# Second attention layer: QKV groups and transpositions of its first two chunks placed in another order

## Chip, core and metric

The kernel runs on one core of one Trainium2 chip. The metric is device time in microseconds (us) of one execution. Times before: 1803.42, 1805.32 and 1803.96 us in three runs, median 1803.96.

## What is computed

`x` is 2048 x 640 floats. Four layers follow one another, each of the form x = x + f(layernorm(x)): attention, Fourier mixing, attention, Fourier mixing.

```python
# attention, layers 0 and 2: 32 heads of 20
qkv = x @ wqkv
idx = pos[:, None] - 2 * arange(8)             # 8 keys, 2 rows apart
logits = einsum("bhsd,bhswd->bhsw", q, k[idx]) * 20 ** -0.5
o = einsum("bhsw,bhswd->bhsd", softmax(logits), v[idx])
y = o @ wo
# mixing, layers 1 and 3
y = dft_seq_re @ (x @ dft_hid_re.T) - dft_seq_im @ (x @ dft_hid_im.T)
```

The change concerns layer 2, the second attention, alone.

## The kernel before

**Tiling.** The rows of x lie in four chunks c (0 to 3) of 512 rows, and each chunk in four tiles j (0 to 3) of 128 rows. The QKV product is cut into 64 groups g: (c, q, j) is chunk, quarter q of the heads, tile. A group is 15 matmuls of 128x480 (`qkv_mm`, L356): every float operand is held as a high and a low part, and three products of five blocks each are summed. Group g writes PSUM bank m0 when g is even and m1 when g is odd, so a group needs its bank emptied by ScalarE first (`qkv_evac`, L363, into the staging tile `stg`, two buffers, two groups per buffer). After each second group the staging tile is stored to HBM: k and v to `kvb` (L372), q to `qb` (L373) (`qkv_store`; the first stores of the layer go by ScalarE's queue, the others by SyncE's, SP).

**Units.** Attention itself runs on VectorE and GpSimd in 32 units u, unit u taking chunk u // 8 and half a quarter of the heads; each unit takes two steps, 2u and 2u + 1. In step s VectorE multiplies q by the keys (`qk_mul`, L425), GpSimd folds the product (L427), VectorE reduces it (L433); ScalarE takes the exponentials of a unit in step 2u + 2 (`soft_exp`, L441); three steps after its L425 VectorE multiplies by the values (`av_mul`, L463) and GpSimd adds the eight products (L478 to L480). A unit reads keys and values as windows from `kvb` (`w_load`, L411) and its q from `qb` (`q_load`, L395), both by SP. `qs` has one buffer; ScalarE copies it into PSUM (`q_copy`, L398, in step 2u - 1), and VectorE's L425 of step 2u waits for that copy.

**Chunks 1 to 3.** Each tile of x is loaded (`x_load`, L189, tag `xa`, two buffers), normalised by ScalarE (`x_norm`, L185, one step ahead of its transposition) and transposed by TensorE (`tp`: transpositions L321, the high part copied by ScalarE L325, subtracted by TensorE L329, the low part copied by ScalarE L344). The output product (`wo_mm`, L503) of chunks 0 and 1 lies between.

**What sets the order.** All of it is written out by hand. `layer_a` puts every piece of work into a plan under a step (from -7 to 66) and a phase, and then issues steps in order and, in each step, the phases of `PHASES` in order. Each engine runs its own instructions in that order, SP its DMAs as well, and a later instruction of an engine never passes an earlier one that waits. The step of group g is `gs[g]`: the first 16 (chunk 0) are listed in `LEAD2`, the others follow from a loop over steps that also sets `tx`, the step in which tile (c, j) is transposed. A group's evacuation stands in the step after it, phase `evac`, if its step is under 6 or odd; in its own step, phase `evacA`, if it is the first of an even step; and in the step after, phase `evacO`, if it is the second. For ScalarE the phases of a step come in the order `evac`, `hi` (L325), `exp` (L441), `evacA`, `actL` (L344), `evacO`, `actl` (L185), `qc` (L398). For SP: `dma` (x_load, q_load), `evac` (early stores), `dmaw` (w_load), `dmas` (weights of the output product, L565, and later stores).

Of the kernel before, what the change touches and what calls it, by code (L numbers as in the profile page):

```python
# [27 lines left out]
NC = 4  # L28
NJ = 4
# [12 lines left out]
LNS = ((40, 52), (40, 52))  # L42


LEAD2 = (-7, -6, -5, -4, -2, 0, 0, 1, 1, 2, 3, 4, 4, 6, 6, 7)
ZTHIRDS = (
    {49: 3, 50: 3, 51: 2, 53: 3, 54: 1, 56: 3, 57: 6, 58: 3, 59: 4, 60: 2, 61: 1, 62: 3, 63: 4, 64: 1, 55: 0, 52: 0},
    {49: 3, 50: 3, 51: 3, 52: 1, 53: 1, 54: 1, 55: 1, 56: 4, 57: 4, 58: 3, 59: 3, 60: 1, 61: 1, 62: 4, 63: 2, 64: 4},
# [25 lines left out]
def tile_layers(ctx: ExitStack, tc: tile.TileContext, x, wqkv, wo, cs, wre, wim, out):  # L74
# [161 lines left out]
    def layer_a(li, stats, handoff, prev):  # L236
        xin, xout = xs[li], xs[li + 1]
        first = li == 0
# [19 lines left out]
        def at(step, phase, fn, *args):  # L258
            plan.setdefault((step, phase), []).append((fn, args))
# [32 lines left out]
        def tp(step, kind, c, j, k0, k1, bank, col=0, tag=None):  # L292
            if step not in pieces:
                pieces[step] = []
                at(step, "peT0", pc_pe, step)
                at(step, "hi", pc_hi, step)
                at(step, "peL", pc_sub, step)
                at(step, "actL", pc_lo, step)
            pieces[step].append((kind, c, j, k0, k1, bank, col, tag))
# [386 lines left out]
        ]  # L686
        gs = list(LEAD0 if first else LEAD2)
        tx = {(0, j): -8 for j in range(NJ)}
        st = 4
        while len(gs) < NGRP:  # L690
            if st % 2 == 0 and len(tx) < NC * NJ:
                c, j = divmod(len(tx), NJ)
                used = [i for i, x in enumerate(order) if x[0] == c - 1 and x[2] == j]
                if used[-1] < len(gs) and gs[used[-1]] < st:
                    tx[(c, j)] = st
            cap = 0 if st < 6 else 2 if st % 2 == 0 and st not in THIN[ly] else 1
            for _ in range(max(0, cap - gs[:16].count(st))):
                if len(gs) < NGRP and len(gs) <= 16 + st and tx.get(order[len(gs)][::2], st) < st:
                    gs.append(st)
            st += 1  # L700
        for g, cqj in enumerate(order):
            st = gs[g]
# [26 lines left out]
        for c in range(1, NC):  # L729
            for j in range(NJ):  # L730
                b = tx[(c, j)]
                at(b - 4, "dma", x_load, c, j)
                if first:
                    at(b - 3, "actl", x_stats, c, j)
                    at(b - 2, "fin", x_fin, c, j)
                at(b - 1, "actl", x_norm, c, j)
                tp(b, "x", c, j, 0, 4, "xt", 0, f"s{j}")
                tp(b, "x", c, j, 4, 5, "t1", 256)
# [538 lines left out]
    st0 = [None] * NC  # L1277
    b1, b2 = LayerB(1), LayerB(3)
    layer_a(0, st0, b1, None)
    st2 = [None] * NC  # L1280
    b1.run(st2)
    layer_a(2, st2, b2, b1)
    b2.run(None)
    b2.ytile(NT - 1, 0, None)
# [56 lines left out]
```

## Time and profile before

| | |
|---|---|
| median of the runs | 1803.96 us |
| the profiled execution's own time | 1805.26 us |
| its span on the core | 1803.4 us |
| what lies around the span | 1.9 us |
| granted TensorE clock over the span | 0.994 |
| TensorE busy | 1743.7 us, 97% |
| VectorE busy | 1382.3 us, 77% |
| GpSimd busy | 633.5 us, 35% |
| ScalarE busy | 816.8 us, 45% |

Layer 2's attention lies in about 890 to 1250 us of the span. In the views below, PE is TensorE (PEld its weight loads), DVE VectorE, ACT ScalarE, POOL GpSimd, SP SyncE, and SPq the DMAs that SP issues. A row of the timeline has the start in us, the length in us, engine, line, operation, the program's names (out <- in), shapes and how many instructions were merged; in square brackets stands how long the engine had been idle before, and which instruction released it. A row of the table by stretches has the stretch, its length, the busy time of each engine with the number of instructions, the granted clock, the share of DMA engines busy and GB/s. The chain of waits gives start, length and what the end of the program waited for.

### The profile page before, as it was taken

How to read it: one execution, taken by the hardware profiler on the slowest of the kernel's cores; microseconds unless marked ns; L12 is line 12 of the kernel's file. 1: busy time of each engine (PE TensorE's matmuls, PEld its weight loads, DVE VectorE, ACT ScalarE, POOL GpSimd, SP SyncE). 2: the span in 40 equal slices, each digit the busy share in tenths (PEclk: the TensorE clock that was granted, in tenths of full speed). 3: DMA queues.
4: the chain of work that ended last, by engine and by line, in shares of the span. 5: the costliest groups of instructions: out<-in, count | busy, mean ns of one | idle time of the engine just before them, and what ended most of it. 6: DMA issues, size and time to landing. Idle time of an engine off the chain costs nothing.

```text
span 1803.4 us, 26465 instructions
## 1 busy us (share of the span) xinstructions
PE 1743.7 (97%) x8798; PEld 1505.7 (83%) x8798; DVE 1382.3 (77%) x2129; ACT 816.8 (45%) x1702; POOL 633.5 (35%) x591
## 2 busy tenths in 40 slices
PE   9999997989999999999999999999899999999999
PEld 6878896877888888888888889878787888888888
DVE  5999899887767767767739987889777676676673
ACT  5654544444445445445523434444534443443441
POOL 3899898950000000000018987899300000000000
PEclk9999998999999999999999999999999999999999
DMA  6896667847777787777647766687687766866861
GB/s 238 280 312 209 211 202 245 273 166 280 261 253 254 247 269 253 240 269 256 224 134 232 258 191 194 204 307 260 205 300 264 251 222 228 266 231 221 261 208 52
DMA packets 271849, 425.15 MB, mean 236 GB/s; under 512 B 22592, under 2 KB 150592, under 8 KB 271456
## 3 DMA queue, kind: packets, MB, share of 16 engines
q1 hardware_dynamic: 268512, 421.49, 70.5%
q10 hardware_dynamic: 3200, 1.97, 0.4%
q8 instruction: 70, 1.15, 0.3%
q14 instruction: 67, 0.55, 0.1%
HBM read 338.23 MB, written 85.14 MB: 235 GB/s over the span
## 4 chain that ended last, share of the span: by engine, by line
PE 64%; DVE 13%; DMA 9%; POOL 7%; issue 3%; ACT 3%; SPq 0%; DVEq 0%; ACTq 0%; POOLq 0%
PE m L356 15%; PE aux L1018 12%; PE t L1107 10%; PE m L1107 10%; PE pq L1107 5%; PE xt L1107 5%; PE aux L503 4%; DMA win<-cs_in 3%; DVE pr L425 2%; POOL pr L478 2%; DVE pr L463 2%; DMA xc<-stg 2%; POOL pr L427 2%; POOL r L876 1%; POOL pr L479 1%
## 5 line engine op out<-in xcount | busy, mean ns | idle before, releaser
L356 PE MATMUL m<-r,s 128*128 128x480 f32 x1920 | 438.3, 383 | 7.5 <-ACT stg L363 2.9
L356 PEld LDWEIGHTS m<-r,s 128*128 128x128 f32 x1920 | 355.9, 188 | 63.4 <-ACT stg L363 4.6
L1100 ACT CAST r<-win 128x512 fp32r<-128x512 f32 x248 | 151.6, 620 | 170.4 <-DVE win L1136 79.9
L168 POOL TENSOR_TENSOR stats<-stats,mhalf 128x1 f32<-128x1 f32 (+1 forms) x40 | 28.8, 719 | 564.5 <-ACT stats L164 564.5
L1018 PE MATMUL aux<-r2a,zo 128*128 128x320 f32 x768 | 226.4, 309 | 0.0
L478 POOL TENSOR_TENSOR pr<-pr 128x640 f32<-128x640 f32 x126 | 205.6, 1632 | 40.1 <-DVE pr L463 39.2
L1018 PE MATMUL aux<-pr,zo 128*128 128x320 f32 x704 | 208.2, 308 | 0.0
L425 DVE TENSOR_TENSOR pr<-pq,win 128x1280 f32<-128x1280 f32 x128 | 189.8, 1483 | 23.4 <-ACT pq L398 23.3
L1101 DVE TENSOR_TENSOR r<-win,r 128x512 fp32r<-128x512 f32 x248 | 167.3, 687 | 45.6 <-ACT r L1100 43.9
L463 DVE TENSOR_TENSOR pr<-pq,win 128x1280 f32<-128x1280 f32 x128 | 190.8, 1491 | 4.3
L427 POOL TENSOR_TENSOR pr<-pr 128x640 f32<-128x640 f32 x128 | 183.5, 1434 | 19.1 <-DVE pr L425 16.1
L1107 PE MATMUL m<-r,r 128*128 128x512 f32 x606 | 156.5, 392 | 1.0 <-DVE r L1101 0.9
L1018 PEld LDWEIGHTS aux<-r2a,zo 128*128 128x128 f32 x768 | 144.1, 188 | 2.0
L940 PE MATMUL m<-s,r 128*128 128x512 f32 x384 | 120.0, 400 | 16.6 <-DMA s<-c0b 5.3
L1107 PEld LDWEIGHTS m<-r,r 128*128 128x128 f32 x606 | 113.5, 188 | 26.9 <-DVE r L1101 1.2
L1018 PEld LDWEIGHTS aux<-pr,zo 128*128 128x128 f32 x704 | 132.2, 188 | 2.1
L1107 PE MATMUL t<-r,r 128*128 128x512 f32 x483 | 130.7, 393 | 2.1 <-issue 2.1
L940 PE MATMUL t<-s,r 128*128 128x512 f32 x384 | 118.1, 395 | 2.3 <-DVE ot L1000 1.5
L479 POOL TENSOR_TENSOR pr<-pr 128x320 f32<-128x320 f32 x126 | 113.7, 903 | 9.9
L363 ACT COPY stg<-m 128x480 f32<-128x480 f32 x128 | 71.1, 556 | 100.7 <-PE m L356 89.9
L433 DVE TENSOR_REDUCE lg<-pr 128x64 f32<-128x640 f32 x128 | 103.9, 812 | 13.8 <-POOL pr L427 13.6
L1107 PEld LDWEIGHTS t<-r,r 128*128 128x128 f32 x483 | 90.5, 188 | 23.6 <-issue 1.5
(274 smaller groups left out, 3231.2 us busy)
## 6 DMA issues: line engine op xcount, KB each, us to landing
win<-cs_in SPq DMA_DIRECT2D x354, 256.0 KB, 4.1
r<-xc SPq DMA_DIRECT2D x240, 256.0 KB, 4.2
win<-kvb SPq DMA_DIRECT2D x96, 440.0 KB, 4.7
xa<-cs_in SPq DMA_DIRECT2D x122, 256.0 KB, 3.9
win<-kvb SPq DMA_DIRECT2D x64, 360.0 KB, 5.1
xc<-stg SPq DMA_DIRECT2D x40, 512.0 KB, 4.6
kvb<-stg SPq DMA_DIRECT2D x60, 320.0 KB, 3.2
xr<-xs SPq DMA_DIRECT2D x40, 320.0 KB, 3.9
```

The lines of the kernel that those rows point to most:

```text
L356: nc.tensor.matmul(mt[g][:, : 3 * F], st[:, a, k], wq[q][:, b, k], start=n == 0, stop=n == 14)
L425: nc.vector.tensor_tensor(pr, q, wview(u, jp, 0, [[1, FE]]), op=ALU.mult)
L427: nc.gpsimd.tensor_tensor(pv[:, :, 0:10], pv[:, :, 0:10], pv[:, :, 10:20], op=ALU.add)
L433: nc.vector.tensor_reduce(lgs[u][:, 2 * jp : 2 * jp + 2].rearrange("p j w h -> p (j w h)"), prq.pop((u, jp))[:, :, 0:10], axis=AX.X, op=AL ...
L463: nc.vector.tensor_tensor(pr.rearrange("p j w (h d) -> p j w h d", d=DH), lgs[u][:, 2 * jp : 2 * jp + 2].unsqueeze(4).to_broadcast([P, 2, ...
L478: g.tensor_tensor(pr[:, :, 0:4], pr[:, :, 0:4], pr[:, :, 4:8], op=ALU.add)
L479: g.tensor_tensor(pr[:, :, 0:2], pr[:, :, 0:2], pr[:, :, 2:4], op=ALU.add)
L940: self.last = nc.tensor.matmul(self.z[t][k], self.xn[c][:, a, j, k * P : (k + 1) * P], self.ct[s][:, b], start=s == 0 and i == 0, stop=s = ...
L1018: self.last = nc.tensor.matmul(self.ym[e][:, :320], zt[(k, a, ri)][:, j2 * P : (j2 + 1) * P], w[:, e * 320 : (e + 1) * 320], start=(k, a, ...
L1100: nc.scalar.copy(hi, raw)
L1101: nc.vector.tensor_tensor(lo, raw, hi.bitcast(F32), op=ALU.subtract)
L1107: nc.tensor.matmul(bank, w(a, kb), hl[b], start=start and (a, b) == (0, 0), stop=stop and (a, b) == (1, 0),)
```

## The change

The core of the diff:

```diff
-LEAD2 = (-7, -6, -5, -4, -2, 0, 0, 1, 1, 2, 3, 4, 4, 6, 6, 7)
+LEAD2 = (-7, -6, -5, -4, -2, -1, 0, 0, 1, 2, 3, 4, 4, 5, 6, 7)
...
-            if st % 2 == 0 and len(tx) < NC * NJ:
+            if (st % 2 == 0 if first or st > 10 else st > 4 and st != 6) and len(tx) < NC * NJ:
...
-                at(b - 4, "dma", x_load, c, j)
+                at(max(b - 4, tx.get((c, j - 2), 0)), "dma", x_load, c, j)
```

What follows from it in layer 2 (layer 0 is as before):

| | before | after |
|---|---|---|
| steps of groups 5, 7, 13 | 0, 1, 6 | -1, 0, 5 |
| steps of groups 14, 15 | 6, 7 | 6, 7 |
| steps of groups 16 to 24 | 8, 9, 10, 10, 11, 13, 14, 14, 15 | 6, 8, 8, 9, 10, 10, 11, 12, 13 |
| groups done by the end of step 21 | 0 to 31 | 0 to 34 |
| groups done by the end of step 33 | 0 to 46 | 0 to 49 |
| the last groups, 60 to 63 | 44, 45, 46, 47 | 44, 45, 46, 47 |
| transpositions of chunk 1 | 6, 8, 10, 12 | 5, 7, 8, 9 |
| of chunk 2 | 18, 20, 22, 24 | 16, 18, 20, 22 |
| of chunk 3 | 32, 34, 36, 38 | 28, 30, 32, 34 |

In the plan group 16 now stands in step 6, after group 14 and ahead of group 15, which is in step 7. So TensorE's order is 13, 14, 16, 15, 17, 18, 19: groups 14 and 16 follow one another on bank m0, and 15 and 17 on m1. Loads that before stood ahead of a store of what they read (the q of unit 2 in step 2; the window and the q of unit 8 in step 14) now stand behind it and wait until it has landed. The units' own steps, the output product and everything from step 48 on keep their places. No instruction is added or removed.

## The prediction

> **What bounds the kernel now.** First the table by stretches, over the attention of layer 2, whose steps 0 to 54 lie in 937 to 1212 us.
>
> ```profile
> 934.00:962.00 28.00, 26.49 (x126) 22.71 (x125) 21.70 (x29) 9.20 (x20) 17.48 (x16) 1.00 0.67 220
> 962.00:1034.00 72.00, 69.56 (x334) 60.09 (x333) 69.37 (x93) 28.81 (x67) 67.41 (x63) 0.98 0.80 258
> 1034.00:1101.00 67.00, 67.00 (x357) 60.23 (x356) 56.45 (x80) 26.29 (x68) 55.69 (x52) 1.00 0.58 187
> 1101.00:1169.00 68.00, 68.00 (x365) 61.11 (x364) 57.72 (x86) 30.74 (x77) 55.88 (x51) 1.00 0.63 201
> 1169.00:1200.00 31.00, 27.34 (x143) 23.39 (x142) 29.87 (x46) 12.78 (x34) 27.39 (x26) 0.97 0.90 290
> ```
>
> The first two numbers behind the length are TensorE's and its weight loads', then VectorE, ScalarE, GpSimd. From 1034 to 1169 TensorE is never idle and VectorE has slack (57.72 of 68). In 962 to 1034 both are full (69.56 and 69.37 of 72). After 1169 VectorE bounds (29.87 of 31). So until step 46 the time is TensorE's work, which the change keeps, plus TensorE's gaps, which it can change. The timeline of TensorE has all gaps of 934 to 1169 that release a matmul late:
>
> ```profile
> 933.68 26.14 PE L356 MATMUL m<-r,s 128*128 128x480 f32 x120
> 961.33 0.66 PE L321 MATMUL xt<-ident,xa 128*128 128x128 f32 x4 [1.51 <-ACT xa L185]
> 961.83 0.27 PE L321 MATMUL t<-ident,xa 128*128 128x128 f32 x1
> 961.86 3.47 PE L356 MATMUL m<-r,s 128*128 128x480 f32 x15
> 965.17 0.39 PE L329 MATMUL xt<-s,nident 128*128 128x512 f32 x1
> 965.40 0.22 PE L329 MATMUL t<-s,nident 128*128 128x128 f32 x1
> 965.46 6.75 PE L356 MATMUL m<-r,s 128*128 128x480 f32 x30
> ...
> 990.59 0.27 PE L321 MATMUL t<-ident,xa 128*128 128x128 f32 x1
> 993.31 0.80 PE L329 MATMUL xt<-s,nident 128*128 128x512 f32 x1 [2.44 <-ACT s L325]
> 993.90 0.31 PE L329 MATMUL t<-s,nident 128*128 128x128 f32 x1
> 994.01 20.92 PE L356 MATMUL m<-r,s 128*128 128x480 f32 x90
> ```
>
> A group costs 26.14 / 8 = 3.27 us; 90 matmuls should take 19.6, the 90 behind the second gap took 20.92, 1.3 more. The clock says why, and the chain of waits where the gap came from:
>
> ```profile
> 994.00:996.00 2.00, 2.00 (x7) 1.72 (x6) 1.54 (x4) 0.75 (x2) 1.84 (x3) 0.50 0.94 372
> ```
>
> ```profile
> 974.89 6.85 DMA qb<-stg
> ...
> 983.94 8.17 DMA qb<-stg
> ...
> 992.21 0.56 ACT stg L363
> 992.77 0.50 ACT s L325
> ...
> 993.31 0.80 PE xt L329
> ```
>
> The store of groups 14 and 15 landed late (6.85 us), SP held the q of unit 6 back for it, the next store went late and took 8.17, and ScalarE could not empty group 20 into its staging buffer; the transposed tile queued behind it, and step 12 had no group to cover for it.
>
> **The change part by part.**
>
> *Removed.* The 1.51: tile (1,0) is normalised one step earlier. The 2.44 with its 1.3 of clock: step 12 gets a group and no transposition. Together 5.25 us, the most that the change can give; there is no other gap up to 1169.
>
> *Moved within TensorE.* The work is the same, but order and banks are new: 14 and 16 both write m0, 15 and 17 both m1. The second of a pair waits until ScalarE has emptied the first, and ScalarE works in its own order. Its pieces, and VectorE's steps 4, 6, 8, 10, 22, 34 and 46, from the two timelines:
>
> ```profile
> 943.64 0.56 ACT L363 COPY stg<-m 128x480 f32<-128x480 f32 x1 [2.38 <-PE m L356]
> 959.90 0.56 ACT L363 COPY stg<-m 128x480 f32<-128x480 f32 x1 [2.72 <-PE m L356]
> 960.36 0.92 ACT L185 ACTIVATE xa<-xa,stats 128x640 f32<-128x640 f32 x1
> 961.18 0.43 ACT L398 COPY pq<-qs 128x320 f32<-128x320 f32 x1
> ...
> 965.50 0.31 ACT L441 ACTIVATE lg<-lg 128x128 f32<-128x128 f32 x1 [2.72 <-DVE lg L452]
> 965.72 0.54 ACT L363 COPY stg<-m 128x480 f32<-128x480 f32 x1
> 966.16 0.59 ACT L344 CAST s<-xt 128x512 fp32r<-128x512 f32 x1
> 966.64 0.28 ACT L344 CAST s<-t 128x128 fp32r<-128x128 f32 x1
> ```
>
> ```profile
> 951.50 1.48 DVE L425 TENSOR_TENSOR pr<-pq,win 128x1280 f32<-128x1280 f32 x1
> ...
> 961.64 1.49 DVE L425 TENSOR_TENSOR pr<-pq,win 128x1280 f32<-128x1280 f32 x1 [0.75 <-ACT pq L398]
> ...
> 970.76 1.49 DVE L425 TENSOR_TENSOR pr<-pq,win 128x1280 f32<-128x1280 f32 x1
> ...
> 979.98 1.48 DVE L425 TENSOR_TENSOR pr<-pq,win 128x1280 f32<-128x1280 f32 x1
> ...
> 1035.17 1.48 DVE L425 TENSOR_TENSOR pr<-pq,win 128x1280 f32<-128x1280 f32 x1
> ...
> 1101.61 1.49 DVE L425 TENSOR_TENSOR pr<-pq,win 128x1280 f32<-128x1280 f32 x1 [2.84 <-ACT pq L398]
> ...
> 1169.31 1.49 DVE L425 TENSOR_TENSOR pr<-pq,win 128x1280 f32<-128x1280 f32 x1
> ```
>
> From these rows: VectorE's step begins 0.46 after its q copy; the exponential starts 3.86 after the step (965.50 - 961.64), the evacuation behind it ends at 4.62; a transposition set delays the next group by 0.53, its subtraction by 0.29; two low copies take 0.76, a normalisation 0.92 (0.82 until the next starts); an evacuation starts 0.15 after its group ends (943.64 against 933.68 + 3 x 3.27). X is the start of VectorE's step 6 in the changed kernel. Step 5 now has a transposition, and its low copies stand ahead of unit 3's q copy on ScalarE, so X is 1.6 after the subtraction of step 5 begins (0.4 subtraction, 0.7 copies, 0.46). Group 14 starts at X - 1.3 and ends at X + 1.96. Then, in us after X, following both orders:
>
> - 3.86 exponential of step 6, 4.62 group 14 emptied. Group 16 from 4.65 to 7.92: **gap 2.7**.
> - 8.63 group 16 emptied; only then tile (1,1) is normalised, ready 9.45. Transposition at 9.5: **gap 1.6**. Group 15 to 13.3, subtraction to 13.6.
> - Low copies to 14.55, normalisation of (1,2) to 15.4, q copy of unit 4, so VectorE's step 8 at 15.7, where before it was 9.12 (970.76 - 961.64). Transposition of step 8 at 15.4: **gap 1.8**. Group 15 emptied 16.2, behind the q copy; group 17 at 16.25: **gap 0.3**.
> - Group 17 to 19.5, subtraction, 18 to 23.1, transposition, 19 to 27.0, subtraction 27.25. Group 18 is emptied behind the low copies of step 9, at 28.55; group 20 at 28.6: **gap 1.35**. VectorE's step 10 at 28.9, before 18.3.
>
> New gaps 7.75. They come from rows of the same kind, so I give them 6 to 10. Does the clock fall again? Behind 1.51 us of gap the stretch 962 to 1034 shows none of its own; behind 2.44 it cost 1.3. The first new gap is 2.7, the nearest row is the 2.44: 1.3, with bounds of 0 and 3.9 (three gaps). The Trainium skill ("TensorE: Matmul & The Clock Gate", Part 1: The HAM clock gate) says that the clock halves after an idle window of about 3.4 us. The measured 0.50 agrees with the halving, but it came after 2.44 us. By the page's window no new gap would cost clock, and the sum would be 1.3 less.
>
> TensorE alone therefore: 7.75 + 1.3 - 5.25 = **+3.8 us**.
>
> *The loads that now wait.* The q of unit 2 waits for the store of groups 6 and 7, and its key window stands behind it on SP. ScalarE also takes unit 1's q copy behind group 7 (943.64) instead of ahead of it, which makes step 2 later. With a store of 6.85 step 4 starts some 3.5 us later than the 951.50 of before; step 6 is held by ScalarE until X anyway (about 965.5, 4 later), so this costs 0, and up to 3 with the 8.17. In step 8 SP holds the store of group 17 until the group is emptied, with unit 4's value window behind it; that window is needed three steps on. x_load of (1,3) waits in step 7 for the transposition of (1,1), its user is normalised 11 us later. Cost 0. No DMA is added.
>
> *VectorE's slack.* VectorE is some 14 us late at step 10 and runs full up to step 22 (9.2 per unit), TensorE too. By the end of step 33 TensorE has done 3 groups and 2 transposition sets more than before: 3 x 3.27 + 2 x 0.82 = 11.45. It bounds there, so step 34 starts at 1101.61 + 11.45 + 3.8 = 1116.9. From 34 to 46 TensorE has 11.45 less to do than the 67.7 of before (1169.31 - 1101.61), 56.25, and VectorE becomes the bound: its 57.72 of 68, so 57.5 in 67.7, at the 69.37 / 72 = 0.963 that it reaches when full, are 59.7. Step 46 at 1176.6, **+7.3 us**. Bounds: +3.8 if TensorE alone counted, +10 if VectorE filled only 0.92 of its time. From step 46 on nothing is moved and VectorE bounds, so the shift goes to the end.
>
> Sum: the profiled execution took 1805.26 us (span 1803.4); it would take 1812.6. The median is 1.3 lower: **1811.3 us**.
>
> **The rivals.**
>
> *Faster: the gaps stay covered.* The place is TensorE between groups 14 and 20. If its new idle time there, clock included, is under 5.25 us, the removed stalls win. This needs ScalarE to empty group 14 before it is held by the exponential, which needs VectorE's step 6 to begin 1.9 us or more ahead of X. Without new gaps: 1803.96 - 5.25 = 1798.7. For it: before, TensorE ran from 961.86 to 990.59 without a gap at the same tightness. Against: X hangs on TensorE's own subtraction of step 5, so VectorE cannot be ahead.
>
> *About the same: TensorE's slip is smaller and VectorE follows.* With gaps of 5 to 6 without loss of clock and VectorE at its 57.5, the time is 1804 to 1806. For it: 1.3 of the price is clock. Against: VectorE has 11.45 us less of cover in the last 12 steps.
>
> *Slower still: the late store again.* Groups 18 and 19 are stored in step 10, behind a weight load as before, and group 22 needs the staging buffer. If that store and the one behind it take 8.17, or two more gaps cost 1.3 each, TensorE loses 3 to 6 more: 1815 to 1818.
>
> *The change doesn't do what it says.* In the changed order each load stands behind the stores of what it reads; the price is the waits above, none of which leads. Here it would give no time of its own.
>
> **How the numbers follow.** Forecast, slower by 4 to 11 us: 0.64. Later stores, slower by 11 to 15: 0.17. About the same: 0.12. Faster: 0.07. A measurement of this kernel tells 0.2%, 3.6 us, from no change. Slower by more 0.81, within 0.12, faster 0.07. The range leaves out the faster rival (0.07), the part of "the same" under the median (0.04) and the end of the late stores (0.05): 1804 to 1817.5.
>
> **What would show it.** In the changed profile TensorE's group 16 waits 2 to 3 us for ScalarE's L363, and there are four gaps of 1 to 3 us between steps 6 and 10, the clock under 1.00 behind the first; the 2.44 before L329 is gone. Step 8 begins 15 to 16 us after step 6 and step 10 some 13 after that. Step 22 is about 15 later than its 1035.17, step 34 15 later, step 46 only 7; VectorE is over 0.94 busy between 34 and 46, with gaps on TensorE there. It is wrong if TensorE runs from step 6 to 10 without gaps, if step 46 is within 3.6 us of 1169.3, or if what follows step 46 takes back the shift.

## The result

Five runs of the changed kernel gave 1810.16 to 1814.18 us, median 1812.98; five of the kernel before, beside them, 1800.97 to 1805.32, median 1803.42. The ratio is 1.0052, with a 95% interval from 1.0037 to 1.0067: 9.4 us slower, 6.7 to 12.1. Forecast were 1811.3 and +7.3.

The profiled execution took 1814.18 us with a span of 1812.3. The table by stretches of the changed kernel's profile, same stretches and columns as shown of before (stretch, length, TensorE, weight loads, VectorE, ScalarE, GpSimd, clock, DMA share, GB/s):

```profile
934.00:962.00 28.00, 28.00 (x137) 24.59 (x136) 19.73 (x28) 8.19 (x18) 14.06 (x13) 1.00 0.58 186
962.00:1034.00 72.00, 64.59 (x302) 54.43 (x301) 54.31 (x73) 23.62 (x54) 53.20 (x50) 0.98 0.70 215
1034.00:1101.00 67.00, 67.00 (x351) 59.51 (x350) 59.64 (x81) 28.78 (x75) 57.88 (x54) 1.00 0.67 214
1101.00:1169.00 68.00, 68.00 (x372) 61.68 (x371) 61.07 (x93) 27.89 (x71) 58.30 (x55) 1.00 0.65 201
```

In 962 to 1034 TensorE lost 5 us of busy time against before and VectorE 15. The timeline of TensorE there (start, length, what; in brackets the idle time before and what ended it):

```profile
936.43 26.15 PE L356 MATMUL m<-r,s 128*128 128x480 f32 x120
...
966.51 3.45 PE L356 MATMUL m<-r,s 128*128 128x480 f32 x15
972.45 5.08 PE L356 MATMUL m<-r,s 128*128 128x480 f32 x15 [2.49 <-ACT stg L363]
979.04 0.65 PE L321 MATMUL xt<-ident,xa 128*128 128x128 f32 x4 [1.51 <-ACT xa L185]
...
984.97 0.66 PE L321 MATMUL xt<-ident,xa 128*128 128x128 f32 x4 [1.60 <-ACT xa L185]
...
998.26 23.04 PE L356 MATMUL m<-r,s 128*128 128x480 f32 x105 [1.25 <-ACT stg L363]
1021.81 3.52 PE L356 MATMUL m<-r,s 128*128 128x480 f32 x15 [0.52 <-ACT stg L363]
```

966.51 is group 14, 972.45 group 16, 979.04 and 984.97 the transpositions of tiles (1,1) and (1,2), 998.26 group 20. The two gaps of before are gone; in their place stand five of 2.49, 1.51, 1.60, 1.25 and 0.52. Group 16 takes 5.08 us where group 14 takes 3.45, and the granted clock says why. It falls to 0.50, called the half clock below:

```profile
972.00:974.00 2.00, 1.55 (x5) 1.35 (x6) 1.90 (x3) 0.39 (x1) 1.91 (x2) 0.78 0.32 129
974.00:976.00 2.00, 2.00 (x6) 1.66 (x5) 1.93 (x4) 0.00 (x0) 1.89 (x2) 0.50 0.00 0
976.00:978.00 2.00, 1.53 (x6) 0.93 (x4) 0.98 (x2) 0.39 (x1) 1.59 (x2) 0.87 0.00 0
```

What held the bank is in ScalarE's timeline, row by row: unit 3's q copy, group 13's evacuation, a wait of 3.42 us for VectorE ahead of the exponential of step 6, and only behind it group 14's evacuation; then group 16's, and only behind that the normalisation of tile (1,1).

```profile
967.29 0.45 ACT L398 COPY pq<-qs 128x320 f32<-128x320 f32 x1
967.65 0.57 ACT L363 COPY stg<-m 128x480 f32<-128x480 f32 x1
971.64 0.31 ACT L441 ACTIVATE lg<-lg 128x128 f32<-128x128 f32 x1 [3.42 <-DVE lg L452]
971.85 0.54 ACT L363 COPY stg<-m 128x480 f32<-128x480 f32 x1
977.61 0.56 ACT L363 COPY stg<-m 128x480 f32<-128x480 f32 x1 [5.22 <-PE m L356]
978.07 0.92 ACT L185 ACTIVATE xa<-xa,stats 128x640 f32<-128x640 f32 x1
```

VectorE's steps 6, 8, 10, 34 and 46, from its timeline; 8.30 and 4.09 us of idle time stand ahead of steps 8 and 10:

```profile
967.77 1.49 DVE L425 TENSOR_TENSOR pr<-pq,win 128x1280 f32<-128x1280 f32 x1 [3.38 <-ACT pq L398]
...
985.28 1.49 DVE L425 TENSOR_TENSOR pr<-pq,win 128x1280 f32<-128x1280 f32 x1 [8.30 <-ACT pq L398]
...
998.57 1.49 DVE L425 TENSOR_TENSOR pr<-pq,win 128x1280 f32<-128x1280 f32 x1 [4.09 <-ACT pq L398]
...
1120.39 1.49 DVE L425 TENSOR_TENSOR pr<-pq,win 128x1280 f32<-128x1280 f32 x1 [2.87 <-ACT pq L398]
...
1180.55 1.48 DVE L425 TENSOR_TENSOR pr<-pq,win 128x1280 f32<-128x1280 f32 x1
```

Group 5 starts at 936.43 here and at 933.68 in the profile of before, though no instruction differs up to there. So steps are counted from the start of group 5, in each profile from its own. The table gives the start of each step's L425, in us from there:

| profile | group 5 at | step 6 | 8 | 10 | 22 | 34 | 46 | 34 to 46 |
|---|---|---|---|---|---|---|---|---|
| before | 933.68 | 27.96 | 37.08 | 46.30 | 101.49 | 167.93 | 235.63 | 67.70 |
| changed | 936.43 | 31.34 | 48.85 | 62.14 | 117.25 | 183.96 | 244.12 | 60.16 |
| changed, second profile | 939.16 | 31.33 | 48.84 | 62.13 | 117.26 | 183.96 | 244.13 | 60.17 |
| banks exchanged | 936.70 | 31.30 | 44.52 | 57.49 | 112.57 | 179.33 | 239.52 | 60.19 |
| before, loads behind stores | 935.30 | 27.95 | 37.06 | 46.29 | 101.36 | 167.29 | 234.99 | 67.70 |
| filler ahead of group 16 | 939.78 | 31.32 | 47.31 | 60.60 | 115.67 | 182.41 | 242.59 | 60.18 |
| limited steps | 935.23 | 31.33 | 47.28 | 60.56 | 115.60 | 173.82 | 241.56 | 67.74 |
| banks and limited steps | 938.43 | 31.30 | 44.52 | 57.53 | 112.57 | 170.78 | 238.52 | 67.74 |
| and normalisations forward | 935.49 | 31.32 | 42.01 | 54.84 | 109.89 | 168.11 | 235.84 | 67.73 |
| and the limit at 20 to 30 | 937.33 | 31.32 | 41.99 | 54.78 | 109.86 | 165.91 | 233.08 | 67.17 |

The changed kernel is 15.8 us late at step 10 and 16.0 at step 34, of which 11.45 is work of TensorE done earlier; at step 46 it is 8.5 late.

### The profile page after: what moved, and what is told of

It reads as the page before. It is cut to its first block, busy times and chain, and to the rows that moved or that the text cites. A ratio compares the mean times of both kernels' runs of the same rounds, so it can differ in the third digit from the quotient of the medians.

```text
span 1812.3 us, 26472 instructions
## 1 busy us (share of the span) xinstructions
PE 1749.5 (97%) x8798; PEld 1507.8 (83%) x8798; DVE 1382.3 (76%) x2129; ACT 815.3 (45%) x1702; POOL 632.4 (35%) x591
## 4 chain that ended last, share of the span: by engine, by line
PE 66%; DVE 13%; POOL 8%; DMA 7%; issue 3%; ACT 3%; SPq 0%; DVEq 0%; ACTq 0%; POOLq 0%
PE m L356 14%; PE aux L1018 13%; PE m L1107 10%; PE t L1107 10%; PE pq L1107 5%; PE xt L1107 5%; PE aux L503 3%; DVE pr L425 3%; DMA win<-cs_in 2%; DVE pr L463 2%; POOL pr L478 2%; POOL pr L427 2%; PE m L940 2%; PE t L940 2%; POOL pr L479 1%
## 5 line engine op out<-in xcount | busy, mean ns | idle before, releaser
L425 DVE TENSOR_TENSOR pr<-pq,win 128x1280 f32<-128x1280 f32 x128 | 189.8, 1483 | 37.9 <-ACT pq L398 37.9
L1136 DVE TENSOR_TENSOR win<-win,win 128x512 f32<-128x512 f32 x110 | 75.6, 690 | 40.6 <-DMA win<-cs_in 38.8
```

What stands on the lines that cost most here:

```text
L425: nc.vector.tensor_tensor(pr, q, wview(u, jp, 0, [[1, FE]]), op=ALU.mult)
```

## The experiments

The theory: the loss has two parts. TensorE loses time in steps 6 to 10, where groups and transpositions wait for work that ScalarE does behind something else; and what it has done too early by step 34 isn't given back in full, because VectorE bounds the last twelve steps. The main rival: the loads that now wait for stores cost the time. Each ratio below is to runs of the kernel before on the same chip; the first four kernels ran on one chip, the last four on another.

**Two banks exchanged.** In the changed kernel, groups 15 and 16 swap m0 and m1; nothing moves.

```diff
-            mt[g] = pt([P, 512], f"m{g % 2}")
+            mt[g] = pt([P, 512], f"m{(g + (not first and g in (15, 16))) % 2}")
```

> The changed kernel with one thing else: groups 15 and 16 exchange their PSUM banks (group 16 on m1, group 15 on m0), so that no two groups that follow one another on TensorE share a bank; the order of every engine stays. Theory (the time is lost where group 16 waits for group 14's bank, held by ScalarE behind an exponential): the 2.5 us gap ahead of group 16 goes, with it the half clock behind it (1.6) and 0.3 ahead of group 17; the normalisation of tile (1,1) comes some 4 us sooner, step 8 about 13 us after step 6 instead of 17.5. TensorE bounds up to step 34, so some 4.5 us come back: 1808 to 1809, about half of the loss. Rival 1 (the loads that wait for stores hold SP and the units): no change, 1813. Rival 2 (only the last twelve steps matter, where VectorE bounds): no change either.

Measured: 1.0016 of the kernel before, interval 1.0005 to 1.0026, where the changed kernel has 1.0052 (1.0037 to 1.0067). TensorE's timeline has groups 14 and 16 back to back, with neither gap nor half clock:

```profile
966.74 6.73 PE L356 MATMUL m<-r,s 128*128 128x480 f32 x30
974.98 0.66 PE L321 MATMUL xt<-ident,xa 128*128 128x128 f32 x4 [1.51 <-ACT xa L185]
...
980.91 0.66 PE L321 MATMUL xt<-ident,xa 128*128 128x128 f32 x4 [1.60 <-ACT xa L185]
```

Step 8 comes 13.2 us after step 6 instead of 17.5, and step 46 is 4.6 earlier (244.12 to 239.52), as expected. Counted at step 46, the bank order alone is about half of the loss (4.6 of 8.5 us); neither rival's "no change" holds. The two gaps behind normalisations stay, and the last twelve steps still take 60.2.

**The waits alone.** In the kernel before, three loads are put behind the stores of what they read.

```diff
-                at(2 * u - 2, "dmaw", w_load, u, 0)
+                at(2 * u - 2, "misc" if not first and u == 8 else "dmaw", w_load, u, 0)
...
-            at(2 * u - 2, "dma", q_load, u)
+            at(2 * u - 2, ("dmaw" if u == 2 else "misc") if not first and u in (2, 8) else "dma", q_load, u)
```

> The kernel before with one thing else: the q load of unit 2, and the window and q loads of unit 8, are put behind the stores of what they read; no group or transposition moves. It is the waits of the change alone. Theory (they are hidden): 0 to +1 us against the kernel before, under 0.1%. Rival 1 (the waits cost the time): +5 to +10 us, most of what the whole change costs.

Measured: 0.9995, interval 0.9985 to 1.0005, no loss, and step 46 is 0.64 us earlier than before. The rival falls for these three loads: standing behind their stores costs 0.9 us at the most (1.0005). The other waits of SP that the change brings, a held store in step 8 and the later load of tile (1,3), were not tested alone. The gap ahead of L329 was 1.17 us here, not 2.44, with two small ones behind; the late store of before is no fixed size.

```profile
993.62 0.50 PE L329 MATMUL xt<-s,nident 128*128 128x512 f32 x1 [1.17 <-ACT s L325]
...
1004.84 9.98 PE L356 MATMUL m<-r,s 128*128 128x480 f32 x45 [0.72 <-ACT stg L363]
```

**The gap filled.** In the changed kernel, eleven more matmuls ahead of group 16, into a bank whose content is not used.

```diff
+            if not first and g == 16:
+                fb = pt([P, 512], "aux0")
+                for i in range(11):
+                    nc.tensor.matmul(fb[:, : 3 * F], xnT[(0, 2, 1)][:, 0, 0], wq[3][:, 0, 0], start=i == 0, stop=i == 10)
```

> The changed kernel with eleven more matmuls of 128x480 on TensorE between groups 14 and 16, into a bank that nobody reads: some 2.4 us of work in the gap of 2.49. Theory (the half clock in group 16 follows from the idle gap): group 16 takes 3.3 to 3.5 us instead of 5.08, so 1.6 us come back: about 1811. If the clock fell for another reason, group 16 stays at about 5 and the time at 1813. If the filler runs past the gap it adds what it overhangs.

```profile
973.15 2.55 PE L353 MATMUL aux<-r,s 128*128 128x480 f32 x11
975.77 3.56 PE L360 MATMUL m<-r,s 128*128 128x480 f32 x15
```

Measured: group 16 (L360 here, four lines on) takes 3.56 us, and step 46 comes 1.5 us earlier than in the changed kernel, which is the clock's share. The whole time, 1.0034 with an interval of 1.0022 to 1.0046, agrees but can't tell 1.6 us from none. That the filler kept the clock up is not shown: the next kernel has the gap of 2.49 us and no filler, and its step 8 (47.28) stands where it stands here (47.31).

**Limited steps.** In the changed kernel, fewer groups from step 18 to 28, so that from step 34 on all stands as before. `THIN` lists the even steps that take one group in place of two; 18, 22 and 26 are new in it, the others of 18 to 28 stood there already.

```diff
-THIN = (..., (12, 16, 20, 24, 28, 32, 36, 44, 48))
+THIN = (..., (12, 16, 18, 20, 22, 24, 26, 28, 32, 36, 44, 48))
```

> The changed kernel with steps 18, 20, 22, 26 and 28 limited to one group each (THIN), so that from step 34 on groups and transpositions stand exactly as in the kernel before; steps up to 17 stay as changed. Theory (the second part of the loss is that TensorE has done three groups too many by step 34 and VectorE bounds the last twelve steps): step 34 comes about 11 us sooner, the stretch from 34 to 46 takes 67 to 68 us instead of 60, and 3 to 4 us come back: 1809 to 1810. Rival (only the gaps of steps 6 to 10 count, and VectorE is late whatever comes behind): no change, 1813.

Measured: 1.0031, interval 1.0019 to 1.0043. Steps 34 to 46 take 67.74 us and step 34 comes 10.1 earlier: both as expected. Against the kernel before, this one is 5.9 us late at step 34 and 5.9 at step 46, so it loses nothing more in the last twelve steps. The changed kernel, its 11.45 of early work taken off, is 4.6 late at step 34 and 8.5 at step 46: what it did too early costs 3.9 there. Step 46 is only 2.6 us earlier than in the changed kernel. Some 1.5 of that is the missing half clock, which the edit comes too late to explain, and 1.0 is the edit's own, less than the 3 to 4 expected, because it brought two gaps (1.16 and 1.38 below). The whole time overlaps with the changed kernel's.

```profile
971.23 3.52 PE L356 MATMUL m<-r,s 128*128 128x480 f32 x15 [2.49 <-ACT stg L363]
...
1038.64 0.66 PE L321 MATMUL xt<-ident,xa 128*128 128x128 f32 x4 [1.16 <-ACT xa L185]
...
1048.47 0.66 PE L321 MATMUL xt<-ident,xa 128*128 128x128 f32 x4 [1.38 <-ACT xa L185]
```

A surprise is in the first of these rows: the same 2.49 us ahead of group 16, in a program that is the same up to there, and no half clock behind it. So the half clock is part of the loss in some executions and not in others.

**Both edits.** The changed kernel with the exchanged banks and the limited steps, the two diffs above.

> The changed kernel with both edits that each gave time back: the banks of groups 15 and 16 exchanged, and steps 18, 20, 22, 26 and 28 limited to one group each. Theory (the loss is the bank wait with its clock, plus VectorE's bound in the last twelve steps, and nothing else): the first edit alone ended at step 46 3.9 us behind the kernel before (counted from group 5), the second alone 5.9; together the gaps left on TensorE are 1.51 + 1.60 + 1.25 + 0.3 + 0.5 + 2.5 ahead of steps 18 to 22 against 5.25 before, so 0 to +2.5 us against the kernel before. Rival (a third cost that neither touches): +4 us or more.

Measured: 1.0018, interval 1.0008 to 1.0029; step 46 is 2.9 us later than before, a little over the 0 to 2.5 expected. The gaps in its timeline are 1.51, 1.60, 1.25, 0.49, 1.16 and 1.41, in sum 7.4, with 0.3 ahead of group 17 gone; less the 5.25 of before that is 2.2. No third cost of 4 us is there; these gaps leave 0.7 us unplaced.

**Normalisations forward.** Both edits, and chunk 1's tiles are normalised in the phase of the exponential, ahead of `evacA` and `evacO`.

```diff
-                at(b - 1, "actl", x_norm, c, j)
+                at(b - 1, "exp" if not first and c == 1 else "actl", x_norm, c, j)
```

> As the kernel with both edits, and chunk 1's normalisations stand one place further forward on ScalarE: behind the exponential of their step (ahead of the evacuation), not behind the evacuation and the low copies. Theory (the gaps of 1.51 and 1.60 are the transpositions waiting for a normalisation that queues behind an evacuation): both gaps go, step 8 comes 11 us after step 6 instead of 13 to 17, and the time is 3 us under the kernel with both edits, 0 to 3 us under the kernel before. If the gaps stay or move behind group 15, it is the same as the kernel with both edits.

```profile
965.55 6.73 PE L356 MATMUL m<-r,s 128*128 128x480 f32 x30
...
972.58 3.53 PE L356 MATMUL m<-r,s 128*128 128x480 f32 x15
...
977.01 0.66 PE L321 MATMUL xt<-ident,xa 128*128 128x128 f32 x4 [0.62 <-ACT s L344]
```

Measured: 0.9997, interval 0.9987 to 1.0006; step 8 is 10.7 us after step 6, step 46 2.7 earlier than with both edits. The gap of 1.51 is gone, of the 1.60 there are 0.62 left, now behind the low copies of the tile before.

**The limit later.** The same, with another list: step 18 has its second group again, and step 30 has one.

```diff
-THIN = (..., (12, 16, 18, 20, 22, 24, 26, 28, 32, 36, 44, 48))
+THIN = (..., (12, 16, 20, 22, 24, 26, 28, 30, 32, 36, 44, 48))
```

> As the kernel with the earlier normalisations, but the steps limited to one group are 20, 22, 24, 26, 28 and 30 instead of 18 to 28: step 18 keeps its second group. Theory: the gaps of 1.16 and 1.38 us ahead of steps 18 to 22, which came with the limit at 18, go too; TensorE has as many groups done by step 33 as in the kernel before: 1 to 2 us under the kernel with the limit at 18, and 2 to 4 under the kernel before.

Measured: 0.9986, interval 0.9976 to 0.9996: 2.5 us faster than the kernel before (0.7 to 4.3), and the loads still stand behind their stores. The gaps ahead of steps 18 to 22 are gone, and step 46 is 2.6 us earlier than before. It has the lowest ratio of the kernels here, though its interval overlaps with that of the kernel above (0.9987 to 1.0006) and of the waits alone.

**The changed kernel again,** with no edit.

> The changed kernel once more, unaltered, on the same chip as the others. Theory: 8 to 10 us over the kernel before, as it was first measured. Its profile also tells whether the half clock behind the 2.49 us gap comes every time: if group 16 takes 3.5 us here as it did in the kernel with the limited steps, the clock is not a fixed part of the loss, and the time varies by 1.6.

Measured: 1.0043, interval 1.0030 to 1.0056, some 7.8 us, which overlaps the first measurement. On the same chip the kernel with the limit at 20 to 30 had 0.9976 to 0.9996, so that one beats the changed kernel as well as the one before. Step for step the second profile repeats the first within 0.02 us from step 6 to 46, and the half clock came again:

```profile
975.16 5.09 PE L356 MATMUL m<-r,s 128*128 128x480 f32 x15 [2.49 <-ACT stg L363]
```

## Why the prediction was right, point by point

- **Removed, 5.25 us.** The gaps of 1.51 and 2.44 are gone from the changed profile. The 2.44 was priced as fixed; with the same order of groups it was 1.17 in another profile.
- **New gaps, 7.75 us** in five: 2.7, 1.6, 1.8, 0.3, 1.35. Measured 2.49, 1.51, 1.60, 0.3 (985.79 less 984.97, less the 0.53 of the transpositions) and 1.25: 7.15. A sixth, 0.52 ahead of group 27, was left out. That they come from the bank is shown for the first and the 0.3 (banks exchanged), and that they come from the place of the normalisation for the next two (normalisations forward). The 1.25 ahead of group 20 is in every profile of the changed order; no run tests its cause.
- **Clock, 1.3 us.** Measured 5.08 - 3.47 = 1.6 in both profiles of the changed kernel, and nothing behind the same gap in the kernel with limited steps. The 1.3 was itself too small for the kernel before: the subtraction behind the 2.44 ran at the half clock too, 0.80 us where 0.39 is usual, so the change removed 0.4 more than the 5.25. As an idle time after which the clock halves, the window of about 3.4 us that the Trainium skill names ("TensorE: Matmul & The Clock Gate", Part 1: The HAM clock gate) does not agree with a clock of 0.50 behind 2.49 us.
- **TensorE alone, +3.8.** Step 34 came at 183.96 against 167.93, less 11.45: +4.6. The gaps and the clock as measured make 7.67 + 1.6 - 5.25 - 0.4 = 3.6. The rest is in how a gap is counted: a bracket starts at the modelled end of the last matmul, though in a row without gaps the next would have started some 0.2 us earlier (a group alone is 3.45 long, one of eight in a row 26.15 / 8 = 3.27). Counted from the start of one row to the start of the next, with 3.27 for a group, TensorE lost 10.1 us here and 5.7 before, half clock included: 4.5 more, which is the 4.6.
- **Step 8, 15.7 after step 6.** It came 17.5 after it: the chain was written without the clock, which was added to the sum alone.
- **Waits of the loads, 0.** Shown by the experiment for the three loads. The detail was wrong: step 4 was to start 3.5 us later and started 0.8 later (18.58 against 17.82), in the second profile 1.5; the store that the q load waits for was out of the way in under 3 us. Step 6 was held by ScalarE at 31.3 in every kernel of the changed order, as priced.
- **VectorE's bound, 59.7 us for steps 34 to 46.** Measured 60.16. The table of that stretch has VectorE at 57.80 of 60.10, 0.962; assumed was 0.963.

```profile
1120.40:1180.50 60.10, 59.53 (x316) 53.19 (x315) 57.80 (x86) 25.51 (x64) 53.80 (x49) 1.00 0.69 211
```

- **Gaps on TensorE in the last twelve steps** were forecast as a sign, and that was wrong: it is busy 59.53 of 60.10 there. It had slack to run ahead. The rows of the transpositions of steps 34 and 46, in the changed kernel and then in the one before:

```profile
1119.61 0.60 PE L321 MATMUL xt<-ident,xa 128*128 128x128 f32 x4
...
1175.32 0.71 PE L321 MATMUL t<-ident,zo 128*128 128x128 f32 x5
```

```profile
1100.89 0.60 PE L321 MATMUL xt<-ident,xa 128*128 128x128 f32 x4
...
1168.14 0.71 PE L321 MATMUL t<-ident,zo 128*128 128x128 f32 x5
```

TensorE went from step 34 to 46 in 55.71 us, VectorE in 60.16: TensorE's lead grew from 0.8 to 5.2 us, and VectorE had no wait for TensorE behind step 34. Before it was 67.25 and 67.70, the lead stayed near 1 us, and VectorE waited 2.8 us for L503. So TensorE's "busy", 1.00 before and 0.99 here, does not tell who bounds. VectorE's share does, 0.85 before and 0.96 here, and so do the lead and the waits.

- **Step 46, +7.3.** Measured +8.5 in both profiles. Too small were TensorE's net loss, by 0.8, and VectorE's stretch, by 0.5. So the mechanism is the forecast one, a little undersized.
- **From step 46 to the end, 0.** From group 5 to the end of the span the changed kernel took 875.87 us against 869.72, +6.15, and 876.64 in its second profile. So up to 2.3 us came back behind step 46. The stretch from step 46 to the end lies between 631.1 and 634.8 us in the ten profiles, with and without the change; whether the change has a part in that stays open. The forecast named such a return as a sign against it, and part of it came. The two misses have opposite signs, so part of the agreement of the total is luck.

## What to carry to other kernels

When pieces of work are moved past each other by hand, look at who frees what they write: two groups that alternate between two banks stop alternating as soon as one is pulled ahead of another, and then the second waits for everything that stands ahead of the evacuation in that engine's order. A moved step takes its preparation along, a normalisation or a copy, and each has a place in another engine's queue that has to move too. Work done earlier on the bounding engine is worth something only if the engine that takes over as the bound can use it; here three groups too many by step 34 left VectorE to set the last twelve steps, at a cost of 3.9 us.

## What the runs showed of the hardware

- The clock behind an idle gap is not settled by the gap's length. Behind 2.49 us on TensorE it fell to 0.50 in both profiles of the changed kernel, and stayed at 1.00 in the kernel with limited steps, which runs the same program up to that place. The rows of the second profile and of the kernel with limited steps:

```profile
975.00:977.00 2.00, 1.84 (x8) 1.58 (x9) 1.90 (x4) 0.11 (x1) 1.84 (x3) 0.93 0.18 72
977.00:979.00 2.00, 2.00 (x7) 1.65 (x6) 1.93 (x4) 0.00 (x0) 1.69 (x2) 0.50 0.00 0
979.00:981.00 2.00, 1.25 (x4) 0.51 (x2) 0.69 (x1) 0.67 (x2) 1.88 (x2) 0.72 0.00 0
```

```profile
971.00:973.00 2.00, 1.77 (x8) 1.56 (x9) 1.90 (x4) 0.18 (x1) 1.84 (x3) 1.00 0.26 106
973.00:975.00 2.00, 1.76 (x9) 1.18 (x7) 1.93 (x4) 0.16 (x1) 1.77 (x2) 1.00 0.00 0
```

- The half clock lasted the same time each time it came here, 3.4 us: 0.3 + 2.0 + 1.1 by the second profile's rows (0.93, 0.50 and 0.72 of 2 us each), 0.9 + 2.0 + 0.5 by the three rows of the first. In stretches of 0.1 us it runs from 973.1 to 976.5, in the second profile from 976.7 to 980.1, and in the kernel before from 993.2 to 996.6. Half of 3.4, 1.7 us, is what it can cost TensorE at the most, by estimate; the measured costs are 1.6 and, in the kernel before, 1.3 + 0.4.
- It did not begin with the matmul that ended the gap: it began 0.7 us behind the start of group 16 (972.45) in the first profile, 1.5 behind it (975.16) in the second, and 0.1 ahead of the subtraction (993.31) in the kernel before. What sets it off stays open.
- Profiles of programs that are the same up to group 5 reached it between 933.68 and 939.78 us, 6 us apart, while steps 6 to 46 repeat within 0.02 us in the two profiles of the changed kernel. A span alone would have mixed that into the result.
